# Backward layer-norm rows from x as loaded, with the scheduler's costs rewritten

## The chip, the cores and the metric

The kernel runs on one core of one Trainium2 chip. The metric is the device time of one execution in microseconds (us), lower is better. All engine names are those of the profile: PE is TensorE's matmul, PEld its weight load, DVE is VectorE, ACT is ScalarE, POOL is GpSimd, SP is SyncE.

## The reference

The reference computes a block of two residual layers and all its gradients. With x of 2048 rows (S) by 448 columns (D), in bfloat16:

```python
h  = x + irfft2(rfft2(layernorm(x)) * (w_r + 1j * w_i))     # a 2-D FFT filter over (S, D)
h2 = h + (gelu(layernorm(layernorm(h)).T @ w1 + b1) @ w2 + b2).T   # an MLP along S, F = 1792
return h2, *vjp(grad_out)     # gradients of x, w_r, w_i, w1, b1, w2, b2
```

What matters here is the gradient through the layer norm of x. With g the gradient that comes out of the inverse FFT for one row, r = 1/std and m the mean of that row of x, and n = (x - m) * r its normal form, the gradient of x is

```
gx = r * g  -  r * n * sum(g * n) / D  +  (gradient of the residual)
```

(the mean of g is zero here, because the table `di1` of the inverse transform leaves the constant term out).

## The kernel before

The program is not written in its final order. Every step is handed to a planner, `Plan`, as an operation with the engines it may run on, a planned occupation and a planned latency in us, the buffers that it reads and the buffers that it writes. `Plan.order()` runs a list schedule over all operations with these planned durations: at each step it takes the engine that can start something first, and of the operations that could start there the one with the longest path behind it (a `boost` adds to that length). `Plan.emit()` then writes each engine's instructions in the order found. On the chip each engine runs its own list strictly in order and waits by semaphores, so a planned duration that differs from the real one does not change what is computed, but an engine may then stand at an instruction whose input is late while later ones could have run. The numbers in the code that look like durations (`("DVE", 0.69, 0.77)`, `small()`, `mm()`) are these planned costs; they are not measured by the program.

Buffers come from rings. A ring has a number of slots; an operation that needs a new buffer can only be placed when a slot is free. `k1` (9 slots of one row tile, 128 x 448 bf16) serves the short-lived row tiles; `f2` (3 slots, float32) the copies out of PSUM; `hx` (3 slots) the reloaded rows of x and h; `ps` is the 8 banks of PSUM, with a limit for each kind of use (`sp` 5, `mm` 4, `mw` 8).

The stages, in the order in which they come: x is loaded and normalised (`Norm.stats`, `Norm.close`, `Norm.make`), transformed by rows (`fft_rows`) and by columns (`fft_cols`), multiplied with the filter (`cmul`), and transformed back (`ifft_cols`, `ifft_rows`), which gives h; h is normalised on POOL (`nh.alts`). The MLP follows (the products `ps_mg`, `ps_mp` and, backward, `ps_mm<-du,w1T`). Then the gradient of h goes through `norm_back` row tile by row tile (16 tiles, h = 0 to 15), and the backward FFT runs: `fft_rows`, `fft_cols`, `cmul`, `ifft_cols`, and in the last row loop (L1258) `ifft_rows` and `norm_back` for each of the 16 row tiles. The matmuls of the weight gradients (`ps_mm<-goT,g_t`, gradient of w2, and `ps_mw<-du_t,hlnT`, gradient of w1) depend on nothing in the backward FFT; the planner lays them between its steps.

The last row loop is where the largest part of the change lies. For each row tile it loads x again (`xr`, ring `hx`), turns it into its normal form in place with `nx.make` on POOL (L1262, the instruction itself is L745), takes the inverse transform (`odd` on ACT L939, two `eo` steps on DVE L941 and L943, six matmuls on PE), and calls `norm_back` (L1177):

- L1180, DVE: the product of g, in PSUM, with the normal form, summed over the row and scaled by `rneg` (r times -1/D) into the column `nm2`. The products go to a tile `junk` of ring `k1` that nobody reads. A small instruction that reads the accumulator follows it.
- L1193, ACT: `v` = r * g, from PSUM. (For the rows of h, L1186 and L1189: DVE makes a mean column `nm1`, ACT makes `v` = r * g + nm1.)
- L1196, DVE: `junk` = normal form * nm2 + v.
- L1199, DVE: the result = junk + the residual's gradient.

The columns r and shift (-m * r) of a norm stand in two arrays, `rstd` and `nb`; `Norm.factors` (L750) makes `rneg`. In the forward rows the row sum of h goes to a column `sm` of its own (L1005) and from there to `mv` (L710).

Of the kernel before, what the change touches and what calls it, by code (L numbers as in the profile page):

```python
# [401 lines left out]
def mm(*cols):  # L402
    t = sum(0.002 + 0.4215e-3 * max(n, 64) for n in cols)
    return [("PE", t, t + 0.07)]
# [3 lines left out]
def kernel(  # L408
# [35 lines left out]
    ring("k1", 9, fifo=False)  # L444
# [199 lines left out]
    rstd_x, rstd_h = const("rstd_x", [P, NT], F32), const("rstd_h", [P, NT], F32)  # L644
    nb_x, nb_h = const("nb_x", [P, NT], F32), const("nb_h", [P, NT], F32)
# [19 lines left out]
    class Norm:  # L665
        def __init__(self, nm, src, dst, by, rstd, nb, rneg, scale, eps, back, mirrored=()):
            self.nm, self.src, self.rstd, self.nb, self.rneg = nm, src, rstd, nb, rneg
            self.scale, self.eps, self.back = scale, eps, back
            self.dst, self.by = dst, by
            self.mirrored = mirrored  # L670

        alts = [("DVE", 0.305, 0.39), ("ACT", 0.65, 0.76)]

        def stats(self, h):
            bs = col(6, f"bs_{self.nm}")
            if h % self.by == 0:
                self.mv = col(2 * self.by, f"mv_{self.nm}")
            mv, i, n = self.mv, h % self.by, self.by
            pl.op(on_dve(448, 1.0e-3, 0.07), lambda e, on: e.bn_stats(out=bs[:], in_=self.src[:, h, :]),
                  r=[(self.src, h)], w=[bs])  # L680
            pl.op(small(), lambda e, on: e.bn_aggr(out=mv[:, 2 * i:2 * i + 2], in_=bs[:]), r=[bs], w=[(mv, i)])
            if i == n - 1:
                self.close(h, mv, self.scale)

        def close(self, h, mv, scale):
            n = self.by
            sl = slice(h + 1 - n, h + 1)
            hs = range(h + 1 - n, h + 1)
            v = col(n, f"v_{self.nm}")
            pl.op([("ACT", 0.19, 0.25)], lambda e, on: e.activation(  # L690
                out=v[:], in_=mv[:].rearrange("p (i c) -> p i c", c=2)[:, :, 1], func=ACT.Sqrt, bias=self.eps[:],
                scale=scale), r=[mv, self.eps], w=[v])
            pl.op(small(), lambda e, on: e.reciprocal(out=self.rstd[:, sl], in_=v[:]),
                  r=[v], w=[(self.rstd, k) for k in hs])
            pl.op(small(), lambda e, on: e.scalar_tensor_tensor(  # L695
                out=self.nb[:, sl], in0=mv[:].rearrange("p (i c) -> p i c", c=2)[:, :, 0], scalar=-1.0,
                in1=self.rstd[:, sl], op0=ALU.mult, op1=ALU.mult), r=[mv] + [(self.rstd, k) for k in hs],
                w=[(self.nb, k) for k in hs])
# [6 lines left out]
        def moments(self, h, sm):  # L705

            if h % self.by == 0:
                self.mv = col(2 * self.by, f"mv_{self.nm}")
            mv, i = self.mv, h % self.by
            pl.op(small(), lambda e, on: e.tensor_scalar(out=mv[:, 2 * i:2 * i + 1], in0=sm[:], scalar1=1.0 / D,  # L710
                                                         scalar2=None, op0=ALU.mult), r=[sm], w=[(mv, (i, 0))])
            sq = k1([P, D], "sq")
            pl.op([("ACT", 0.64, 0.8)], lambda e, on: e.activation(
                out=sq[:], in_=self.src[:, h, :], func=ACT.Square, scale=-1.0, bias=mv[:, 2 * i:2 * i + 1],
                accum_out=mv[:, 2 * i + 1:2 * i + 2]), r=[(self.src, h), (mv, (i, 0))], w=[sq, (mv, (i, 1))])
            if i == self.by - 1:
                self.close(h, mv, self.scale / D)

        def make_mirrored(self, h):

            for k in range(2):
                def go(e, on, k=k):
# [4 lines left out]
                    if on == "ACT":  # L727
                        e.activation(out=out, in_=in_, func=ACT.Identity, scale=self.rstd[:, h:h + 1],
                                     bias=self.nb[:, h:h + 1])
                    else:  # L730
                        e.tensor_scalar(out=out, in0=in_, scalar1=self.rstd[:, h:h + 1], scalar2=self.nb[:, h:h + 1],
                                        op0=ALU.mult, op1=ALU.add)
                pl.op([("DVE", 0.2, 0.28), ("ACT", 0.4, 0.5)], go, r=[(self.src, h), (self.rstd, h), (self.nb, h)],
                      w=[(self.dst, (h, k) if k else h)])

        def make(self, dst, h, src=None, at=None):
            s, i = (self.src, h) if src is None else (src, at)
            j = h if src is None else at

            def go(e, on):  # L740
                if on == "ACT":
                    e.activation(out=dst[:, j, 0:D], in_=s[:, i, :], func=ACT.Identity,
                                 scale=self.rstd[:, h:h + 1], bias=self.nb[:, h:h + 1])
                else:
                    e.tensor_scalar(out=dst[:, j, 0:D], in0=s[:, i, :], scalar1=self.rstd[:, h:h + 1],  # L745
                                    scalar2=self.nb[:, h:h + 1], op0=ALU.mult, op1=ALU.add)

            pl.op(self.alts, go, r=[(s, i), (self.rstd, h), (self.nb, h)], w=[(dst, j)])

        def factors(self):  # L750
            pl.op(small(), lambda e, on: e.tensor_scalar(out=self.rneg[:], in0=self.rstd[:], scalar1=self.back,
                                                         scalar2=None, op0=ALU.mult),
                  r=[self.rstd], w=[self.rneg])
# [129 lines left out]
    def ifft_cols(ys, ab):  # L883

        for a in (7, 6, 5, 4, 3, 2, 1, 8):
# [16 lines left out]
            matmuls([pa, pb], calls, rd + [hi], mm(*[128] * (len(calls) // 2)), "rows")  # L902
# [80 lines left out]
    nx = Norm("x", x, xln, 4, rstd_x, nb_x, rneg_x, 1.0, eps_x, -1.0 / D, (0,))  # L983
# [16 lines left out]
    nh = Norm("h", hn, hln, 2, rstd_h, nb_h, rneg_h, 1.0 + LN_EPS, eps_h, -(1.0 + LN_EPS) / D)  # L1000
    nh.alts = [("POOL", 0.95, 1.05)]
    for h in range(NT):
        with grouped():
            py = ifft_rows(ab, di0, h)
            sm = col(1, "sm")  # L1005
            pl.op([("DVE", 0.61, 0.69)], lambda e, on, py=py, h=h, sm=sm: e.tensor_tensor_reduce(
                out=hn[:, h, :], in0=py[:], in1=hn[:, h, :], scale=1.0, scalar=0.0, op0=ALU.add, op1=ALU.add,
                accum_out=sm[:]), r=[py, (hn, h)], w=[(hn, h), sm])
            nh.moments(h, sm)
# [51 lines left out]
    for j in range(NFB):  # L1061
# [28 lines left out]
        gop(on_dve(448, 1.2e-3, 0.07), [kk, hh], [(du, j), (gb1, j)], lambda e, g, j=j: e.scalar_tensor_tensor(  # L1090
# [69 lines left out]
    for t in range(NT):  # L1160
# [3 lines left out]
        pl.op(on_dve(448), lambda e, on, t=t, p2=p2, h2=h2: e.scalar_tensor_tensor(  # L1164
# [5 lines left out]
    for h in range(NT):  # L1170
        pl.op([("ACT", 0.55, 0.65)], lambda e, on, h=h: e.activation(
# [5 lines left out]
    def norm_back(pb, mean, xhat, xkey, h, nm, base, out, okey):  # L1177
        nm2 = col(1, "nm2")
        junk = k1([P, D], "junk")
        pl.op([("DVE", 0.69, 0.77)], lambda e, on: e.tensor_tensor_reduce(  # L1180
            out=junk[:], in0=pb[:, 0:D], in1=xhat(), scale=nm.rneg[:, h:h + 1], scalar=0.0, op0=ALU.mult,
            op1=ALU.add, accum_out=nm2[:]), r=[pb, xkey, nm.rneg], w=[junk, nm2])
        v = pl.buf("f2", [P, D], "v", F32)
        if mean:
            nm1 = col(1, "nm1")
            pl.op(small(), lambda e, on: e.tensor_scalar(  # L1186
                out=nm1[:], in0=pb[:, D:D + 1], scalar1=nm.rstd[:, h:h + 1], scalar2=-1.0 / D, op0=ALU.mult,
                op1=ALU.mult), r=[pb, (nm.rstd, h)], w=[nm1])
            pl.op([("ACT", 0.6, 0.7)], lambda e, on: e.activation(  # L1189
                out=v[:], in_=pb[:, 0:D], func=ACT.Identity, scale=nm.rstd[:, h:h + 1], bias=nm1[:]),  # L1190
                r=[pb, nm1, (nm.rstd, h)], w=[v])
        else:
            pl.op([("ACT", 0.53, 0.63)], lambda e, on: e.activation(  # L1193
                out=v[:], in_=pb[:, 0:D], func=ACT.Copy, scale=nm.rstd[:, h:h + 1]),
                r=[pb, (nm.rstd, h)], w=[v])
        pl.op(on_dve(448, 1.1e-3), lambda e, on: e.scalar_tensor_tensor(  # L1196
            out=junk[:], in0=xhat(), scalar=nm2[:], in1=v[:], op0=ALU.mult, op1=ALU.add), r=[xkey, nm2, v, junk],
            w=[junk])
# [17 lines left out]
    for h in range(NT):  # L1216
        pd = product("mm", D + 1, [(lambda h=h, j=j: w1T[h][0][:, w1T[h][1], j, :], lambda j=j: du[:, j, 0:D + 1],
                                    [w1T[h], (du, j), (du, (j, 1))]) for j in range(NFB)], [P, 512])
        norm_back(pd, True, lambda h=h: hln[:, h, :], (hln, h), h, nh, lambda h=h: go_r[:, h, :],
# [162 lines left out]
```

## Time and profile before

| | |
|---|---|
| runs | 354.47, 354.40, 352.72 us; median 354.40 us |
| the profiled execution | 352.68 us, its span 350.9 us |
| granted TensorE clock | 1.00 |
| PE busy | 329.8 us, 94% of the span |
| DVE busy | 275.0 us, 78% |
| ACT busy | 191.4 us, 55% |
| POOL busy | 83.7 us, 24% |

The span runs from the first to the last instruction; the 1.8 us between it and the execution's time lie around it. The profiled execution lies at the low end of the runs. The page's busy time of PE is the time in which at least one matmul was under way, and its idle time is what is left.

### The profile page before, as it was taken

What the parts mean: (1) busy time and instruction counts of PE and PEld (TensorE: products, weight loads), DVE (VectorE), ACT (ScalarE), POOL (GpSimd) and SP (SyncE); (2) the same over time, 40 slices, a digit from 0 to 9 for tenths busy, and PEclk for the clock granted to TensorE, in tenths of its full rate; (3) what the DMA queues carried; (4) which work ended last, traced back from release to release, by engine and by line L of the source; (5) the groups of instructions that cost most, each with busy time, mean ns of one, the idle gap of its engine ahead of it and who ended that gap; (6) DMA issues with size and microseconds to landing.
All of it is one profiled execution on the core that took longest, in us unless ns stands there. A gap on an engine that the chain in (4) does not pass through costs nothing. (4 is left out here: it accounts for less than half of the span.)

```text
span 350.9 us, 6872 instructions
## 1 busy us (share of the span) xinstructions
PE 329.8 (94%) x2507; PEld 179.8 (51%) x2507; DVE 275.0 (78%) x747; ACT 191.4 (55%) x410; POOL 83.7 (24%) x140
## 2 busy tenths in 40 slices
PE   0979999999999999999999999998999999899994
PEld 0546555677555555555555555654556555444441
DVE  5898999899379994323277887989997989998852
ACT  2596843486487776406012323976878676634332
POOL 0000000056701101033220100050111566355642
PEclk9999999999999999999999999999999999999999
DMA  7999999994999999799799999999996546347755
GB/s 238 384 222 216 179 179 288 223 244 139 358 302 282 355 279 346 182 348 239 194 222 239 186 226 239 225 184 164 150 171 217 178 175 219 143 174 241 220 196 209
DMA packets 134685, 80.49 MB, mean 229 GB/s; under 512 B 94268, under 2 KB 127164, under 8 KB 134524
## 3 DMA queue, kind: packets, MB, share of 16 engines
q1 hardware_dynamic: 127148, 52.71, 70.8%
q0 software_dynamic: 7504, 27.35, 23.3%
q8 instruction: 19, 0.31, 0.4%
q14 instruction: 14, 0.11, 0.1%
HBM read 30.98 MB, written 27.08 MB: 165 GB/s over the span
## 5 line engine op out<-in xcount | busy, mean ns | idle before, releaser
L517 PE MATMUL ps_mm<-goT,g_t 128*128 128x512 bf16 x224 | 55.6, 379 | 0.8 <-DVE nm L1180 0.8
L517 PE MATMUL ps_mg<-go_n,w2T 128*128 128x448 bf16 x224 | 50.3, 357 | 0.8 <-DMA go_n<-in_grad_out_dram 0.8
L517 PE MATMUL ps_mw<-du_t,hlnT 128*128 128x448 bf16 (+1 forms) x256 | 45.4, 353 | 0.5 <-DVE nm L1180 0.3
L517 PE MATMUL ps_mm<-du,w1T 128*128 128x449 bf16 x224 | 43.3, 353 | 0.0
L517 PE MATMUL ps_mp<-hln,w1c 128*128 128x448 bf16 x224 | 42.7, 352 | 0.0
L517 PE MATMUL ps_mp<-gT,w2c 128*128 128x448 bf16 x224 | 42.7, 352 | 0.0
L507 ACT CAST s<-ps_mm 128x512 bf16<-128x512 f32 x56 | 33.1, 602 | 9.7 <-PE ps_mm L517 9.6
L499 POOL DMA_DIRECT2D out_dram<-s x31 | 17.1, 552 | 86.5 <-ACT s L507 70.1
L1189 ACT ACTIVATE v<-ps_mm,nm,rstd_h 128x448 f32<-128x448 f32 x16 | 11.6, 726 | 42.4 <-DVE nm L1186 42.4
L517 PEld LDWEIGHTS <-hlnT 128*128 128x128 bf16 (+1 forms) x256 | 20.5, 97 | 23.8 <-issue 6.6
L517 PEld LDWEIGHTS <-w1T 128*128 128x128 bf16 x224 | 21.8, 97 | 21.1
L517 PEld LDWEIGHTS <-w2c 128*128 128x128 bf16 x224 | 21.9, 98 | 20.5
L517 PEld LDWEIGHTS <-w1c 128*128 128x128 bf16 x224 | 21.9, 98 | 20.5
L507 ACT CAST s<-ps_mw 128x448 bf16<-128x448 f32 x32 | 16.3, 535 | 24.9 <-PE ps_mw L517 22.6
L517 PEld LDWEIGHTS <-g_t 128*128 128x128 bf16 x224 | 19.4, 97 | 19.5 <-issue 2.4
L517 PEld LDWEIGHTS <-w2T 128*128 128x128 bf16 x224 | 19.6, 98 | 15.8 <-issue 1.7
L509 DVE CAST s<-ps_mw 128x448 bf16<-128x448 f32 x32 | 19.2, 620 | 8.8 <-PE ps_mw L517 3.7
L1164 DVE SCALAR_TENSOR_TENSOR h<-ps_mp,b2c,hr 128x448 bf16<-128x448 f32 x16 | 9.8, 677 | 16.6 <-PE ps_mp L517 16.6
L817 DVE TENSOR_TENSOR gg<-ps_sp,gb 128x226 bf16<-128x226 f32 x60 | 20.0, 408 | 3.2 <-ACT gb L507 3.2
L499 POOL DMA_DIRECT2D hn_d<-x x4 | 2.4, 590 | 73.4 <-DVE nb_h L695 72.5
L1077 DVE SCALAR_TENSOR_TENSOR ge<-ge 128x448 bf16<-128x448 bf16 x14 | 8.7, 621 | 14.1 <-ACT ge L1075 14.1
L517 PEld LDWEIGHTS <-kinv 128*128 128x128 bf16 x192 | 14.8, 97 | 8.2 <-DVE eo L943 3.5
(128 smaller groups left out, 590.1 us busy)
## 6 DMA issues: line engine op xcount, KB each, us to landing
w2c<-in_B_w_dram SPq DMA_DIRECT2D x8, 896.0 KB, 9.0
out_dram<-s POOLq DMA_DIRECT2D x14, 512.0 KB, 4.8
out_dram<-s POOLq DMA_DIRECT2D x15, 448.0 KB, 3.0
w1c<-in_B_w_dram SPq DMA_DIRECT2D x6, 1024.0 KB, 11.5
x<-in_A_x_dram SPq DMA_DIRECT2D x4, 448.0 KB, 6.7
go_n<-in_grad_out_dram SPq DMA_DIRECT2D x2, 896.0 KB, 10.6
hn_d<-x POOLq DMA_DIRECT2D x4, 448.0 KB, 6.1
hln_d<-hln POOLq DMA_DIRECT2D x4, 448.0 KB, 7.4
```

The lines of the kernel that those rows point to most:

```text
L499: e.dma_start(out=out() if callable(out) else out, in_=in_())
L507: e.copy(out=out(), in_=in_())
L509: e.tensor_copy(out=out(), in_=in_())
L517: e.matmul(out(), lhsT=lhsT(), rhs=rhs(), start=start, stop=stop)
L817: pl.op(on_dve(226), lambda e, on, s_=s_, op=op: e.tensor_tensor(out=g_[:, s_, :].rearrange("p (k t) -> p t k", t=2), in0=pr[:, 0:2, :], i ...
L1077: gop(stt, [q_, uf], [zz], lambda e, g: e.scalar_tensor_tensor(out=g(zz), in0=g(q_), scalar=6.0 * GELU_C, in1=g(uf), op0=ALU.add, op1=ALU. ...
L1164: pl.op(on_dve(448), lambda e, on, t=t, p2=p2, h2=h2: e.scalar_tensor_tensor(out=h2[:], in0=p2[:, 0:D], scalar=b2c[:, t:t + 1], in1=hr[t / ...
L1189: pl.op([("ACT", 0.6, 0.7)], lambda e, on: e.activation(out=v[:], in_=pb[:, 0:D], func=ACT.Identity, scale=nm.rstd[:, h:h + 1], bias=nm1[: ...
```

## The change

The change has four parts.

1. In the last row loop the normal form of x is no longer made. `norm_back` takes x as loaded. Because the mean of g is zero, sum(g * n) = r * sum(g * x), so `factors` multiplies `rneg` of x by r once more (one instruction for the whole kernel). The column c = sum(g * x) * rneg is then multiplied with the pair (r, shift), which now stand side by side in one array `rn`, by one small DVE instruction on 128 x 2 values; ACT makes v = r * g + shift * c with the function Identity in place of Copy, and DVE adds x * (r * c).
2. The row-sum products (`junk`) get a ring of their own, `jk`, of 2 slots; `k1` goes from 9 slots to 8.
3. `rstd` and `nb` are merged into `rn`; the square root's column becomes a part of `mv`, and so does the row sum `sm` of the forward rows. No instruction is added or removed by this.
4. Planned costs are rewritten: of short matmuls, of the `rows` matmuls of `ifft_cols`, of the row sums, of the fused multiply-adds, of the normalisation on POOL, and of the row sums on ACT. The four sign copies of the table `kf` at the start get a boost of 60.

```diff
 def mm(*cols):
-    t = sum(0.002 + 0.4215e-3 * max(n, 64) for n in cols)
+    t = sum(0.002 + 0.4215e-3 * max(n, 120) for n in cols)
...
-    ring("k1", 9, fifo=False)
+    ring("k1", 8, fifo=False)
+    ring("jk", 2, fifo=False)
...
-            matmuls([pa, pb], calls, rd + [hi], mm(*[128] * (len(calls) // 2)), "rows")
+            matmuls([pa, pb], calls, rd + [hi], mm(*[143] * (len(calls) // 2)), "rows")
...
         def factors(self):
-            pl.op(small(), lambda e, on: e.tensor_scalar(out=self.rneg[:], in0=self.rstd[:], scalar1=self.back,
+            pl.op(small(), lambda e, on: e.tensor_scalar(out=self.rneg[:], in0=self.rn[:, :, 0], scalar1=self.back,
...
+            if self.raw:
+                pl.op(small(), lambda e, on: e.tensor_tensor(out=self.rneg[:], in0=self.rneg[:], in1=self.rn[:, :, 0],
+                                                             op=ALU.mult), r=[self.rn, self.rneg], w=[self.rneg])
...
+    pl.boost = 60.0
     for k, sign in ((1, 1.0), (2, -1.0), (3, -1.0), (4, 1.0)):
-        pl.op([("DVE", 0.1, 0.2)], lambda e, on, k=k, sign=sign: e.tensor_scalar(
+        pl.op([("DVE", 0.118, 0.2)], lambda e, on, k=k, sign=sign: e.tensor_scalar(
             out=kf[:, k, :], in0=kf[:, 0, :], scalar1=sign, scalar2=None, op0=ALU.mult), r=[(kf, 0)], w=[(kf, k)])
+    pl.boost = 0.0
...
+    nx.raw = True
...
-    nh.alts = [("POOL", 0.95, 1.05)]
+    nh.alts = [("POOL", 0.72, 0.78)]
...
-            pl.op([("DVE", 0.61, 0.69)], lambda e, on, py=py, h=h, sm=sm: e.tensor_tensor_reduce(
+            pl.op([("DVE", 0.54, 0.68)], lambda e, on, py=py, h=h, mv=mv, i=i: e.tensor_tensor_reduce(
...
-        pl.op(on_dve(448), lambda e, on, t=t, p2=p2, h2=h2: e.scalar_tensor_tensor(
+        pl.op([("DVE", 0.595, 0.68)], lambda e, on, t=t, p2=p2, h2=h2: e.scalar_tensor_tensor(
...
-        pl.op([("ACT", 0.55, 0.65)], lambda e, on, h=h: e.activation(
+        pl.op([("ACT", 0.70, 0.80)], lambda e, on, h=h: e.activation(
...
-    def norm_back(pb, mean, xhat, xkey, h, nm, base, out, okey):
-        nm2 = col(1, "nm2")
-        junk = k1([P, D], "junk")
-        pl.op([("DVE", 0.69, 0.77)], lambda e, on: e.tensor_tensor_reduce(
+    def norm_back(pb, xhat, xkey, h, nm, base, out, okey):
+        nms = col(3, "nm")
+        junk = pl.buf("jk", [P, D], "junk")
+        pl.op([("DVE", 0.605, 0.73)], lambda e, on: e.tensor_tensor_reduce(
             out=junk[:], in0=pb[:, 0:D], in1=xhat(), scale=nm.rneg[:, h:h + 1], scalar=0.0, op0=ALU.mult,
...
-        if mean:
...
-            pl.op([("ACT", 0.6, 0.7)], lambda e, on: e.activation(
-                out=v[:], in_=pb[:, 0:D], func=ACT.Identity, scale=nm.rstd[:, h:h + 1], bias=nm1[:]),
+        if nm.raw:
+            by = 1
+            pl.op([("DVE", 0.075, 0.17)], lambda e, on: e.tensor_scalar(
+                out=nms[:, 1:3], in0=nm.rn[:, h, :], scalar1=nms[:, 0:1], scalar2=None, op0=ALU.mult),
+                r=[(nms, 0), (nm.rn, (h, 0)), (nm.rn, (h, 1))], w=[(nms, 1), (nms, 2)])
         else:
-            pl.op([("ACT", 0.53, 0.63)], lambda e, on: e.activation(
-                out=v[:], in_=pb[:, 0:D], func=ACT.Copy, scale=nm.rstd[:, h:h + 1]),
+            by = 0
+            pl.op([("DVE", 0.131, 0.213)], lambda e, on: e.tensor_scalar(
+                out=nms[:, 2:3], in0=pb[:, D:D + 1], scalar1=nm.rn[:, h, 0:1], scalar2=-1.0 / D, op0=ALU.mult,
...
-        pl.op(on_dve(448, 1.1e-3), lambda e, on: e.scalar_tensor_tensor(
-            out=junk[:], in0=xhat(), scalar=nm2[:], in1=v[:], op0=ALU.mult, op1=ALU.add), r=[xkey, nm2, v, junk],
+        pl.op([("ACT", 0.53, 0.64)], lambda e, on: e.activation(
+            out=v[:], in_=pb[:, 0:D], func=ACT.Identity, scale=nm.rn[:, h, 0:1], bias=nms[:, 2:3]),
+            r=[pb, (nms, 2), (nm.rn, (h, 0))], w=[v])
+        pl.op([("DVE", 0.595, 0.68)], lambda e, on: e.scalar_tensor_tensor(
+            out=junk[:], in0=xhat(), scalar=nms[:, by:by + 1], in1=v[:], op0=ALU.mult, op1=ALU.add),
...
     gx_op = []
-    nx.alts = nh.alts
     for h in range(NT):
         with grouped():
             py = ifft_rows(ab2, di1, h)
             g = h // 2
-            nx.make(xr[g], h, xr[g], h % 2)
             gx = k1([P, D], "gx")
-            norm_back(py, False, lambda g=g, h=h: xr[g][:, h % 2, :], (xr[g], h % 2), h, nx,
+            norm_back(py, lambda g=g, h=h: xr[g][:, h % 2, :], (xr[g], h % 2), h, nx,
```

More of the change, by code (lines that the diff above doesn't have):

```diff
@@ L642, in ld_w1 @@
                      w1v[:, :, a * P:b_ * P], P * NT * (b_ - a) * P * 2)
-    rstd_x, rstd_h = const("rstd_x", [P, NT], F32), const("rstd_h", [P, NT], F32)
-    nb_x, nb_h = const("nb_x", [P, NT], F32), const("nb_h", [P, NT], F32)
+    rn_x, rn_h = const("rn_x", [P, NT, 2], F32), const("rn_h", [P, NT, 2], F32)
     rneg_x, rneg_h = const("rneg_x", [P, NT], F32), const("rneg_h", [P, NT], F32)
@@ L688, in close @@
             hs = range(h + 1 - n, h + 1)
-            v = col(n, f"v_{self.nm}")
             pl.op([("ACT", 0.19, 0.25)], lambda e, on: e.activation(
[L691 to L694, printed above, removed]
+                out=mv[:, 2 * n:3 * n], in_=mv[:, 1:2 * n:2], func=ACT.Sqrt, bias=self.eps[:],
+                scale=scale), r=[mv, self.eps], w=[(mv, "v")])
+            pl.op(small(), lambda e, on: e.reciprocal(out=self.rn[:, sl, 0], in_=mv[:, 2 * n:3 * n]),
+                  r=[(mv, "v")], w=[(self.rn, (k, 0)) for k in hs])
             pl.op(small(), lambda e, on: e.scalar_tensor_tensor(
-                out=self.nb[:, sl], in0=mv[:].rearrange("p (i c) -> p i c", c=2)[:, :, 0], scalar=-1.0,
-                in1=self.rstd[:, sl], op0=ALU.mult, op1=ALU.mult), r=[mv] + [(self.rstd, k) for k in hs],
-                w=[(self.nb, k) for k in hs])
+                out=self.rn[:, sl, 1], in0=mv[:, 0:2 * n:2], scalar=-1.0,
+                in1=self.rn[:, sl, 0], op0=ALU.mult, op1=ALU.mult), r=[mv] + [(self.rn, (k, 0)) for k in hs],
+                w=[(self.rn, (k, 1)) for k in hs])
             for k in hs:
@@ L727, in go @@
                     if on == "ACT":
-                        e.activation(out=out, in_=in_, func=ACT.Identity, scale=self.rstd[:, h:h + 1],
-                                     bias=self.nb[:, h:h + 1])
+                        e.activation(out=out, in_=in_, func=ACT.Identity, scale=self.rn[:, h, 0:1],
+                                     bias=self.rn[:, h, 1:2])
                     else:
-                        e.tensor_scalar(out=out, in0=in_, scalar1=self.rstd[:, h:h + 1], scalar2=self.nb[:, h:h + 1],
+                        e.tensor_scalar(out=out, in0=in_, scalar1=self.rn[:, h, 0:1], scalar2=self.rn[:, h, 1:2],
@@ L732, in go, with make @@
                                         op0=ALU.mult, op1=ALU.add)
-                pl.op([("DVE", 0.2, 0.28), ("ACT", 0.4, 0.5)], go, r=[(self.src, h), (self.rstd, h), (self.nb, h)],
+                pl.op([("DVE", 0.25, 0.34), ("ACT", 0.46, 0.57)], go, r=[(self.src, h), (self.rn, (h, 0)), (self.rn, (h, 1))],
                       w=[(self.dst, (h, k) if k else h)])
-        def make(self, dst, h, src=None, at=None):
-            s, i = (self.src, h) if src is None else (src, at)
-            j = h if src is None else at
+        def make(self, dst, h):
@@ L740, in go @@
             def go(e, on):
                 if on == "ACT":
-                    e.activation(out=dst[:, j, 0:D], in_=s[:, i, :], func=ACT.Identity,
-                                 scale=self.rstd[:, h:h + 1], bias=self.nb[:, h:h + 1])
-                else:
-                    e.tensor_scalar(out=dst[:, j, 0:D], in0=s[:, i, :], scalar1=self.rstd[:, h:h + 1],
-                                    scalar2=self.nb[:, h:h + 1], op0=ALU.mult, op1=ALU.add)
-            pl.op(self.alts, go, r=[(s, i), (self.rstd, h), (self.nb, h)], w=[(dst, j)])
+                    e.activation(out=dst[:, h, 0:D], in_=self.src[:, h, :], func=ACT.Identity,
+                                 scale=self.rn[:, h, 0:1], bias=self.rn[:, h, 1:2])
+                else:
+                    e.tensor_scalar(out=dst[:, h, 0:D], in0=self.src[:, h, :], scalar1=self.rn[:, h, 0:1],
+                                    scalar2=self.rn[:, h, 1:2], op0=ALU.mult, op1=ALU.add)
@@ L999 @@
     hln = big(1, [P, NT, D], "hln")
[L1000 to L1001 removed]
+    nh = Norm("h", hn, hln, 2, rn_h, rneg_h, 1.0 + LN_EPS, eps_h, -(1.0 + LN_EPS) / D)
+    nh.alts = [("POOL", 0.72, 0.78)]
     for h in range(NT):
@@ L1181, in norm_back @@
             out=junk[:], in0=pb[:, 0:D], in1=xhat(), scale=nm.rneg[:, h:h + 1], scalar=0.0, op0=ALU.mult,
-            op1=ALU.add, accum_out=nm2[:]), r=[pb, xkey, nm.rneg], w=[junk, nm2])
+            op1=ALU.add, accum_out=nms[:, 0:1]), r=[pb, xkey, nm.rneg], w=[junk, (nms, 0)])
         v = pl.buf("f2", [P, D], "v", F32)
-        if mean:
[L1185 to L1188, printed above, removed]
-            pl.op([("ACT", 0.6, 0.7)], lambda e, on: e.activation(
-                out=v[:], in_=pb[:, 0:D], func=ACT.Identity, scale=nm.rstd[:, h:h + 1], bias=nm1[:]),
-                r=[pb, nm1, (nm.rstd, h)], w=[v])
-        else:
-            pl.op([("ACT", 0.53, 0.63)], lambda e, on: e.activation(
-                out=v[:], in_=pb[:, 0:D], func=ACT.Copy, scale=nm.rstd[:, h:h + 1]),
-                r=[pb, (nm.rstd, h)], w=[v])
```

39 lines of the change are left out of this document (21 added, 18 removed).

## The prediction

> **What bounds the kernel.** I read the page's busy times first: PE is the engine that is nearly full, and DVE is the next.
>
> ```profile
> PE 329.8 (94%) x2507; PEld 179.8 (51%) x2507; DVE 275.0 (78%) x747; ACT 191.4 (55%) x410; POOL 83.7 (24%) x140
> ```
>
> The chain that ended last says little more (its last long piece is 26.52 us of PE's `ps_mw`), so the question is where PE stood still. Going through PE's timeline, I add up the gaps between matmuls: the first 8.43 us (waiting for `w2n`'s transfer), then 8.08 us in all. They lie in four places: 2.76 us in the start (0.76 before 11.08, 2.00 before 23.20), 0.83 in the forward column transform, 1.53 around 240, and 2.94 from 275 to 316, in the last row loop. Everything else is matmuls end to end, and 4.6 us behind the last matmul are eviction and store. So an edit is worth what it takes out of these gaps, and no more.
>
> Next I asked for the timeline of each engine around the gap at 240. First PE, then DVE, then POOL:
>
> ```profile
> 238.77 0.38 PE L517 MATMUL ps_sp<-gg,hf 128*64 128x225 bf16 x4
> 240.47 0.69 PE L517 MATMUL ps_sp<-gg,hf 128*64 128x225 bf16 x8 [1.32 <-DVE gg L817]
> ...
> 242.50 0.35 PE L517 MATMUL ps_sp<-gg,hf 128*64 128x225 bf16 x3 [0.21 <-DVE gg L817]
> ```
>
> ```profile
> 233.77 3.34 DVE L860 TENSOR_TENSOR t_r<-ds,w_b 128x1800 bf16<-128x1800 bf16 x1
> 237.03 1.08 DVE L860 TENSOR_TENSOR t_i<-ds,w_b 128x1800 bf16<-128x1800 bf16 x1
> 238.04 1.01 DVE L817 TENSOR_TENSOR gg<-ps_sp,gb 128x226 bf16<-128x226 f32 x3
> ```
>
> ```profile
> 231.95 4.21 POOL L745 TENSOR_SCALAR xr<-xr,rstd_x,nb_x 128x448 bf16<-128x448 bf16 x6
> ```
>
> The same product (`t_r`, `t_i`, 128x1800) takes 3.34 us while POOL is making the normal form of x, and 1.08 us right after. PE waits for a DVE result 1.32 + 0.21 us behind it. Comparing every DVE instruction with the median of its group, I find two more that overlap POOL's L745, both in the last row loop:
>
> ```profile
> 297.00 1.31 DVE L1199 TENSOR_TENSOR gx<-junk,go_r 128x448 bf16<-128x448 bf16 x1
> ```
>
> ```profile
> 297.07 1.67 POOL L745 TENSOR_SCALAR xr<-xr,rstd_x,nb_x 128x448 bf16<-128x448 bf16 x2
> ```
>
> This `gx` takes 1.31 us where its neighbours take 0.38. The third is an L1196 at 282.62 with 0.80 for 0.68. Together POOL's 16 normalisations cost DVE 2.26 + 0.93 + 0.12 = 3.31 us. The chain that ended last runs straight through the second one:
>
> ```profile
> 298.31 0.30 DVE eo L943
> ...
> 300.93 0.09 DVE nm L1180
> 301.02 0.04 issue
> 301.06 1.89 PE ps_mm L517 x8
> ```
>
> The `eo` that PE waits for stands behind the blocked `gx`; PE loses 0.21 us before 298.67 and 0.75 before 301.06.
>
> **The change, part by part.** *POOL's normal form goes (16 x 0.712 us of POOL).* POOL itself is 24% busy and costs nothing; what counts is what DVE gets back. At 240: 1.53 us of PE's idle time. At 297: 0.21 + 0.75 = 0.96. Sum -2.49 us. Why it should reach the end: PE has a fixed amount of matmuls to do, and from 242 to 346 its gaps add up to 3.2 us, so what starts earlier ends earlier. What is late next at 240 is the other input of that matmul, ACT's copy `gb`, and it was itself waiting for DVE (2.34 us idle before 240.50), so it moves up too.
>
> [...]
>
> *One small DVE instruction more for each row tile (128x2).* Nearest rows: `RECIPROCAL rstd_h`, 128x2, lasts 160 ns, but what the queue loses is the distance to the next start, 0.07 to 0.12 us (22.51 to 22.59, 22.88 to 22.94). 16 x 0.08 = 1.3 us of DVE, at most 16 x 0.16 = 2.6. From 270 to 308 DVE is busy 34.6 of 38 us, so it's not free: it gets back 1.05 us there from POOL, so the net is +0.25 us (+1.5 at most). As DVE's own relief there is counted above through PE's gap, I charge +0.2.
>
> [...]
>
> *ACT's `v` now waits for DVE.* Before, L1193 needed PSUM alone and ran beside L1180. Now the row is a chain: L1180 (0.61 to the next start, 0.08 for the accumulator) then the small one (0.15), then `v`, then L1196. Queued behind `v` on ACT are the `odd` copies and the evictions of `ps_mm`, for which PE waits. `v` itself goes from Copy to Identity with a bias column: L1193 has 639 ns, L1189, the same function on the same shape, 724: 16 x 0.085 = 1.4 us of ACT, which is 70% busy there (26 of 38 us), so hidden. The wait is hidden if another row's `eo`, L1196 or L1199 is there for DVE and evictions for ACT: a row period is 2.6 us (L1180 from 270.62 to 309.28 in 15 steps) and the row's chain from L1180 to L1199 some 3.1 us, so two rows must be in flight. The planner knows the dependency and two `jk` slots allow just that. Cost between 0 and 16 x 0.6 us; the nearest row is L1189 itself, which already stands in such a chain in the rows of h with no PE gap; I take +0.3.
>
> *Rings and columns.* `k1` loses a slot but gives up `junk`, of which two were alive at a time: 0. The columns: the same instructions, 0. `factors`: one instruction of 0.17 us for the kernel, 0.
>
> *The start.* The sign copies of `kf` move from behind the second statistics (9.12 to 12.14) to the moment the table lands. They cost DVE 4 x 0.12 us, of which half now sits in the wait after a reciprocal: at most +0.5. In return PE can begin `kf,xln` when the first row is ready (about 10.3 in place of 12.52), without the 0.76 us wait; ACT's `zt` copies and, queued behind them, `v_x` (17.69, DVE idle 1.51 us for it) come earlier, and with them the `w` for which PE stood 2.00 us. Between -2.3 and +0.5; I take -0.5, as `go_n` and `w2T` may hold PE anyway.
>
> *Planned costs.* Each comes nearer to the trace: four 113-column matmuls take 0.21 us (planned 0.198, now 0.210), L1180 0.61 (0.69, now 0.605), L1196 0.60 (0.56, now 0.595), POOL 0.71 (0.95, now 0.72). A better plan should leave fewer of the remaining gaps (0.83 in the columns, 1.98 in the row loop), but a new order is a new draw. -1.5 to +1.5; taken as 0.
>
> Sum: -2.49 + 0.2 + 0.3 - 0.5 = -2.5 us. On the profiled 352.68 that is 350.2; counted from the median of the runs, 354.40, it is 351.9. The profiled execution lies at the low end of the runs (352.72 to 354.47), and a new median may fall anywhere between, so I say 351.0, in the middle.
>
> **Rivals.**
>
> *The new wait shows (slower).* In the last row loop ACT stands at `v` until DVE has done L1180 and the small column, the `odd` copies behind it come late, `eo` is late, and PE stalls as it already does five times on `eo`. For: two of 16 `v` waited for DVE already (1.5 us). Against: PE has `ps_mw` to fill with, ACT has 30% to spare. If half the rows lose 0.76 + 0.15 us, that's 8 x 0.91 = 7.3, less the 2.5 gained: 352.7 + 4.8 = 357.5. It decides from 3 rows in 16, where 2.7 eats the gain. If five rows are hit, 4.5 - 2.5 = +2.0: 354.7 from the profiled time, 356.4 from the median.
>
> *The lock is gone but nothing arrives.* The gap at 240 closes, but the planner places other work so that PE waits elsewhere, for DVE that has 1.3 us more to do: a gain of 0 to 1.5 from the middle of the two times (353.5): 352.0 to 353.5. For: DVE is 91% busy in the row loop and the order is drawn anew. Against: PE's gap at 240 has one cause, which is gone.
>
> *The start and the better plan pay in full.* -2.49 - 2.3 and another -1 in the row loop, 5.8 in all: 346.9 from the profiled time, 348.6 from the median.
>
> **How the numbers follow.** About 0.5% (1.8 us) is what a measurement of this kernel can tell from no change. The forecast has 0.5, the full gain 0.1, the lock with nothing to show 0.2, the slower one 0.2. Faster takes the first two: 0.6; same 0.2; slower 0.2. The range: the forecast's own is 349 to 353 (the new order 1.5 us each way, the spread of the runs 0.9); the lower end goes to 348.5 for half of the full gain, the upper to 355.5 to take in the slower case with a few rows hit.
>
> **What would show it.** Right: no L745 `xr`; `t_r<-ds,w_b` 128x1800 at about 1.08 us; all L1199 near 0.38; no PE gap over 0.5 us between 230 and 270; 16 small DVE instructions that cost 0.08 each. Wrong: ACT idle before `v` with PE waiting on `eo` for more than the 1.5 us of before in the row loop; PE's gaps over the whole span adding up to 8 us or more again; a gap in the start that grew because DVE did `kf` before its statistics.

## The result, and the profile after

The changed kernel takes 354.79 us (median of 22 executions, 353.76 to 357.71); the kernel before, run beside it on the same chip, 353.07 us (22 executions, 351.92 to 355.84). The ratio is 1.0051 with a 95% interval of 1.0032 to 1.0070: slower by 0.5%, where a gain of 2.5 us was forecast. The profiled execution of after takes 354.65 us with a span of 352.9 us, 2.0 us longer than the span before. The ratios leave out executions over 1.5% above the fastest of the same kernel: three of six of `e3_raw_only` below, one of twelve of `e1_own_column`, no others.

The busy times on the page say that work did move as intended: POOL lost 12.0 us and DVE 4.6 us, and PE still fills 94% of a longer span.

```profile
PE 331.7 (94%) x2507; PEld 180.6 (51%) x2507; DVE 270.4 (77%) x755; ACT 196.8 (56%) x419; POOL 71.7 (20%) x124
```

Where the prediction expected relief, relief came. The groups by form show `t_r` at 1.10 us (3.34 before), `gx` at a mean of 394 ns (442 before), and the new small instruction (columns: busy us, mean ns of one, idle time before):

```profile
L859 DVE TENSOR_TENSOR t_r<-ds,w_b 128x1800 bf16<-128x1800 bf16 x1 | 1.1, 1097 | 0.0
...
L1206 DVE TENSOR_TENSOR gx<-junk,go_r 128x448 bf16<-128x448 bf16 x16 | 6.2, 394 | 0.0
...
L1192 DVE TENSOR_SCALAR nm<-rn_x,nm 128x2 f32<-128x2 f32 x16 | 3.7, 232 | 0.0
```

From 266 to 304, in the last row loop, PE is busy 37.92 of 38 us (35.52 before), and all of PE's gaps behind 226 add up to 0.67 us. Yet PE's gaps behind its first matmul sum to 7.93 us over the whole span, almost the 8.08 of before. What was won at 240 and in the row loop was lost in a place where before had no gap at all. First PE's timeline of before, where the same products follow each other without a wait:

```profile
220.16 0.39 PE L517 MATMUL ps_sp<-kf,w 128*113 128x128 bf16 x4
220.38 0.59 PE L517 MATMUL ps_mm<-goT,g_t 128*128 128x512 bf16 x2
220.81 0.39 PE L517 MATMUL ps_sp<-kf,w 128*113 128x128 bf16 x4
```

And PE's timeline of after; the bracket gives the idle time before an instruction and what ended it:

```profile
220.18 0.38 PE L518 MATMUL ps_sp<-kf,w 128*113 128x128 bf16 x4 [0.16 <-ACT v L1200]
222.89 0.59 PE L518 MATMUL ps_mm<-goT,g_t 128*128 128x512 bf16 x2 [2.33 <-ACT v L1200]
223.37 0.53 PE L518 MATMUL ps_sp<-kf,w 128*113 128x128 bf16 x4
225.59 1.01 PE L518 MATMUL ps_mm<-goT,g_t 128*128 128x512 bf16 x2 [1.69 <-ACT v L1200]
226.39 0.63 PE L518 MATMUL ps_sp<-kf,w 128*113 128x128 bf16 x4
226.82 4.47 PE L518 MATMUL ps_mm<-goT,g_t 128*128 128x512 bf16 x12
```

Two long gaps, 2.33 and 1.69 us, and with the 0.16 ahead of them 4.18 us in all, each ended by `v` (L1200). This is not the `v` of the last row loop, which the prediction feared: it belongs to the rows of h, 50 us earlier, whose code the change hardly touches. Behind the gaps, 12 matmuls take 4.47 us, 0.37 each. The windows of after show why (columns: PE, PEld, DVE, ACT, POOL busy with counts, granted clock, DMA share, GB/s):

```profile
218.00:222.00 4.00, 2.40 (x29) 1.85 (x28) 3.05 (x10) 0.72 (x1) 0.00 (x0) 1.00 0.75 211
222.00:226.00 4.00, 1.42 (x8) 0.73 (x8) 3.09 (x8) 2.39 (x5) 0.00 (x0) 0.68 0.00 0
226.00:229.00 3.00, 3.00 (x12) 1.42 (x11) 3.00 (x9) 2.19 (x6) 0.00 (x0) 0.50 0.49 97
229.00:232.00 3.00, 3.00 (x24) 1.74 (x23) 1.53 (x6) 2.20 (x5) 0.00 (x0) 0.79 1.28 290
```

The granted clock, 1.00 here before, falls to half. So the loss goes on after the gap: in the kernel with the mended plan (`e2_planner_told`) 14 of the same matmuls take 3.18 us, 0.227 each, and 12 x (0.372 - 0.227) = 1.7 us.

Landmarks give the sum. The first matmul starts 0.27 later (8.43 to 8.70); from there to the end of the last `ps_mm<-du,w1T` it is 210.12 before and 210.20 after, +0.08; from there to the end of the last backward `kf,w` 8.76 and 15.04, +6.28; from there to the last matmul 119.05 and 114.40, -4.65. Together +1.98, the difference of the spans to within 0.03.

### The profile page after: what moved, and what is told of

Read it like the earlier page. It is cut to its first block, busy times and chain, and to the rows that moved or that the text cites. A ratio compares the mean times of both kernels' runs of the same rounds, so it can differ in the third digit from the quotient of the medians.

```text
span 352.9 us, 6853 instructions
## 1 busy us (share of the span) xinstructions
PE 331.7 (94%) x2507; PEld 180.6 (51%) x2507; DVE 270.4 (77%) x755; ACT 196.8 (56%) x419; POOL 71.7 (20%) x124
## 5 line engine op out<-in xcount | busy, mean ns | idle before, releaser
L518 PE MATMUL ps_mm<-goT,g_t 128*128 128x512 bf16 x224 | 56.8, 391 | 4.0 <-ACT v L1200 4.0
L518 PE MATMUL ps_mg<-go_n,w2T 128*128 128x448 bf16 x224 | 49.4, 355 | 1.6 <-DMA go_n<-in_grad_out_dram 0.7
L1200 ACT ACTIVATE v<-ps_mm,nm,rn_h 128x448 f32<-128x448 f32 x16 | 11.6, 725 | 48.7 <-DVE nm L1186 46.7
L518 PEld LDWEIGHTS <-g_t 128*128 128x128 bf16 x224 | 20.3, 100 | 25.3 <-issue 7.4
L508 ACT CAST s<-ps_mw 128x448 bf16<-128x448 f32 x38 | 18.6, 538 | 22.9 <-PE ps_mw L518 19.3
L510 DVE CAST s<-ps_mw 128x448 bf16<-128x448 f32 x26 | 15.9, 624 | 10.2 <-PE ps_mw L518 8.3
L1203 DVE SCALAR_TENSOR_TENSOR junk<-hln,nm,v 128x448 bf16<-128x448 bf16 x16 | 10.9, 684 | 11.8 <-ACT v L1200 11.8
```

Of the source, the lines that this page charges most:

```text
L508: e.copy(out=out(), in_=in_())
L510: e.tensor_copy(out=out(), in_=in_())
L518: e.matmul(out(), lhsT=lhsT(), rhs=rhs(), start=start, stop=stop)
L1200: pl.op([("ACT", 0.53, 0.64)], lambda e, on: e.activation(out=v[:], in_=pb[:, 0:D], func=ACT.Identity, scale=nm.rn[:, h, 0:1], bias=nms[:, ...
L1203: pl.op([("DVE", 0.595, 0.68)], lambda e, on: e.scalar_tensor_tensor(out=junk[:], in0=xhat(), scalar=nms[:, by:by + 1], in1=v[:], op0=ALU. ...
```

## Why PE waits at 220

The chain of waits stops at `v`; the question is why `v` is late. In the rows of h, each row tile needs on DVE a row sum, a mean column and, behind ACT's `v`, a fused multiply-add and an addition. DVE also folds finished rows (`u`, `w`, L770 before and L769 after) into the input of `kf,w`. DVE's timeline of before, one row:

```profile
210.71 0.68 DVE L1180 CUSTOM_DVE_ANT_0 junk<-ps_mm,hln,rneg_h 128x448 bf16<-128x448 f32 x1
...
211.45 1.15 DVE L770 TENSOR_TENSOR u<-go_r 128x896 bf16<-128x896 bf16 x2
212.51 0.68 DVE L1196 SCALAR_TENSOR_TENSOR junk<-hln,nm,v 128x448 bf16<-128x448 bf16 x1
...
213.53 0.68 DVE L1180 CUSTOM_DVE_ANT_0 junk<-ps_mm,hln,rneg_h 128x448 bf16<-128x448 f32 x1
```

And a row of after, first on DVE and then ACT's `v` of that row:

```profile
211.97 0.67 DVE L1186 CUSTOM_DVE_ANT_0 junk<-ps_mm,hln,rneg_h 128x448 bf16<-128x448 f32 x1
...
213.53 0.69 DVE L1203 SCALAR_TENSOR_TENSOR junk<-hln,nm,v 128x448 bf16<-128x448 bf16 x1 [0.88 <-ACT v L1200]
214.25 0.39 DVE L1206 TENSOR_TENSOR go_r<-junk,go_r 128x448 bf16<-128x448 bf16 x1
214.68 1.16 DVE L769 TENSOR_TENSOR u<-go_r 128x896 bf16<-128x896 bf16 x2
215.76 0.21 DVE L1197 TENSOR_SCALAR nm<-ps_mm,rn_h 128x1 f32<-128x1 f32 x1
215.88 0.68 DVE L1186 CUSTOM_DVE_ANT_0 junk<-ps_mm,hln,rneg_h 128x448 bf16<-128x448 f32 x1
```

```profile
212.77 0.73 ACT L1200 ACTIVATE v<-ps_mm,nm,rn_h 128x448 f32<-128x448 f32 x1 [1.99 <-DVE nm L1186]
```

In both, some 0.9 us pass between the row sum and the multiply-add, because `v` runs only after the row sum. Before lays the fold `u` in that hole: a row with a fold takes 2.82 us. After leaves the hole empty, waits 0.88 us, and lays the fold between rows: such a row takes 3.91 us. The starts of the 16 row sums of h span 40.53 us before (178.44 to 218.97) and 45.12 us after (178.91 to 224.03). The product that feeds them ends at 218.55 and 218.90. So before is done with the rows as the product ends, and after is two rows behind; by the brackets above, PE's next products start only behind the `v` of those rows, after 0.16, 2.33 and 1.69 us, which fits PSUM banks that the rows still hold.

The order differs because the plan does. In `order()` the longest path behind an operation counts occupations. By the old costs, mean column and `v` (0.075 + 0.60 = 0.675) are shorter than the row sum (0.69), so the row sum comes first and the plan itself sees the hole. By the new ones 0.131 + 0.53 = 0.661 is longer than 0.605: the mean column comes first, and the plan lets `v` run beside the row sum, so that it sees no hole to fill. On the chip `v` doesn't run beside it. The dependency that keeps it back isn't among those the planner was given. (The new costs of row sum and mean column are closer to the trace than the old ones. That of `v` isn't: where ACT goes straight on, its next start comes 0.62 us behind `v`, from 222.12 to 222.74, so 0.60 was the nearer number. With it the sum would be 0.731 and the order the same.)

## The experiments

**Is it the shared column tile?** After puts row sum and mean into one tile, `nms`; before had two. Theory A: `v` waits for the row sum because of the tile. Theory B: it waits whatever the tile.

```diff
-            by = 0
+            by, nm1 = 0, col(1, "nm1", bufs=2)
...
-                out=nms[:, 2:3], in0=pb[:, D:D + 1], ...
+                out=nm1[:], in0=pb[:, D:D + 1], ...
```

The ring of `nms` goes from four columns to three, and `v` takes its bias from the new column; every engine's order is that of after.

> The changed kernel with one edit: in the rows of h the mean column is written to a tile of its own instead of the third column of the tile that L1186's accumulator also writes. Every engine's instructions stay in the same order; only what `v` (L1200) waits for changes. Theory A (the shared tile): `v` waited for L1186 because both columns lie in one tile; with its own column it starts about 0.25 us after the row's product is done in place of 0.9, the DVE row chain goes from 2.72 us to some 2.1, under the 2.67 of the product, so it no longer falls behind; the PE gaps of 2.33 and 1.69 us before the backward FFT and the twelve slow matmuls behind them (1.9 us) go: about 6 us, 347 to 350 us against 353.1 of before. Rival B (two slots for the row-sum products, or the folds placed between the rows): the rows stay at 2.7 us each, the gaps stay, 354 to 355.

Measured: 356.26 us against 354.0 of before, ratio 1.0062 (1.0024 to 1.0099). The gaps stay (0.13 + 2.33 + 1.26). DVE's mean column and row sum, then ACT's `v`, in the timelines of this kernel:

```profile
220.57 0.21 DVE L1197 TENSOR_SCALAR nm<-ps_mm,rn_h 128x1 f32<-128x1 f32 x1
220.70 0.67 DVE L1186 CUSTOM_DVE_ANT_0 junk<-ps_mm,hln,rneg_h 128x448 bf16<-128x448 f32 x1
```

```profile
221.50 0.72 ACT L1200 ACTIVATE v<-ps_mm,nm,rn_h 128x448 f32<-128x448 f32 x1 [1.99 <-DVE nm L1186]
```

The column that `v` reads is made ahead of 220.70, in a tile of its own, and `v` still starts after the row sum. Theory A falls.

**Does it help if the planner knows?** After, with one entry changed in the list of what `v` reads. The instruction and its waits on the chip are the same; the plan now puts `v` behind the row sum.

```diff
-            r=[pb, (nms, 2), (nm.rn, (h, 0))], w=[v])
+            r=[pb, nms, (nm.rn, (h, 0))], w=[v])
```

> The changed kernel with the shared tile kept, but the planner told of it: `v` is listed as reading the whole tile, so the plan has `v` behind L1186. The order changes, the wait remains. Theory A in its full form (not the wait as such, but a plan that does not know of it): the folds go into the wait for `v` as in the kernel before, the last rows of h are not late, PE gaps before the backward FFT under 1 us, 349 to 352 us. If the wait as such is the cost: the rows still fall behind, 354 to 355. Rival B (two slots): as slow as the changed kernel.

Measured: 349.79 us against 354.0, ratio 0.9887 (0.9844 to 0.9931). The fold is back in the hole, in DVE's timeline of this kernel, and the row starts span 40.84 us (178.06 to 218.90):

```profile
210.64 0.68 DVE L1186 CUSTOM_DVE_ANT_0 junk<-ps_mm,hln,rneg_h 128x448 bf16<-128x448 f32 x1
...
211.38 1.15 DVE L769 TENSOR_TENSOR u<-go_r 128x896 bf16<-128x896 bf16 x2
212.44 0.67 DVE L1203 SCALAR_TENSOR_TENSOR junk<-hln,nm,v 128x448 bf16<-128x448 bf16 x1
```

The gap on PE is gone but for 0.11 us and the clock stays at 1.00. `e11_told_again` is the same kernel once more, run beside another experiment:

> e2 once more, unchanged, on the same chip as e10, to compare with. 348 to 350.5 us.

It measured 349.08 against 352.56, 0.9882 (0.9837 to 0.9928). One true dependency in the plan is worth 1.6% (1.0051 to 0.9887).

**By the mean's cost alone.** If the order flipped over 0.661 against 0.605, setting the mean column's occupation back should do as well.

```diff
-            pl.op([("DVE", 0.131, 0.213)], lambda e, on: e.tensor_scalar(
+            pl.op([("DVE", 0.070, 0.213)], lambda e, on: e.tensor_scalar(
```

> The changed kernel with one planned number altered: the mean column of the rows of h (L1197) at 0.070 us of occupation in place of 0.131. Its path (0.070 + 0.53 for `v`) is then shorter than the row sum's 0.605, so the plan puts the row sum first again, as in the kernel before, and `v` behind both. Theory C (DVE's row sum and ACT's `v` read the same PSUM bank and so run one after the other in the order in which they were written; the plan doesn't know, and the new costs made it count on `v` running beside the row sum): the plan is true again, PE gaps before the backward FFT under 1 us, 348.5 to 351 us against 353.5 of before. Rival (the other new costs, or the ring of two slots, hold the rows up): gaps of 3 us or more stay, 355 to 357.

Measured: 349.25 against 353.13, ratio 0.9896 (0.9859 to 0.9933); gaps 0.25 + 0.11 in place of 4.18, row starts over 41.1 us. A planned number that is 0.06 us too low undoes the loss, because it puts the row sum first again.

**What holds `v` back on the chip.** DVE's row sum and `v` read the same PSUM tile. Here `v` of the rows of h takes its input from SBUF (the normal form `hln` stands in for g, so that term is left out of the gradient). The order of every engine is that of `e1_own_column`.

```diff
-            out=v[:], in_=pb[:, 0:D], func=ACT.Identity, ...
+            out=v[:], in_=pb[:, 0:D] if nm.raw else hln[:, h, :], func=ACT.Identity, ...
```

> e1 (the changed kernel with the mean column in a tile of its own, every engine's order unchanged) with `v` in the rows of h reading the normal form of h from SBUF instead of the product in PSUM; the gradient through h's norm is left out that way. Theory C: nothing in PSUM is shared any more, `v` starts when the mean column is there, beside the row sum; DVE's wait of 0.88 us for `v` in each row goes, the rows take at most 2.2 us, the two PE gaps near 220 (3.6 to 4.0 us) go: 347 to 350 us. Rival (it waits for the row sum for another reason: ring slots, DVE's own order): `v` still starts 0.9 us behind, gaps stay, 354 to 357.

Measured: 347.33 against 353.13, ratio 0.9854 (0.9812 to 0.9895). First ACT's timeline, then DVE's:

```profile
213.87 0.76 ACT L1200 ACTIVATE v<-hln,nm,rn_h 128x448 f32<-128x448 bf16 x1 [1.39 <-DVE nm L1197]
```

```profile
213.67 0.68 DVE L1186 CUSTOM_DVE_ANT_0 junk<-ps_mm,hln,rneg_h 128x448 bf16<-128x448 f32 x1
...
214.66 0.68 DVE L1203 SCALAR_TENSOR_TENSOR junk<-hln,nm,v 128x448 bf16<-128x448 bf16 x1 [0.31 <-ACT v L1200]
```

`v` is released by the mean column (L1197) and runs beside the row sum, as the plan had it; the hole shrinks from 0.88 to 0.31, the row starts span 40.2 us, and there is no gap at 220. Over the 16 rows of h, row sum and `v` never overlap in `e1_own_column`; here they do in 15. With the same order, it is the common PSUM tile that keeps `v` back: while both read it they run one after the other, 0.80 us from start to start in `e1_own_column` (220.70 to 221.50), and 0.20 here (213.67 to 213.87). For that row of `e1_own_column` the profile names the row sum's accumulator (L1186) as what ended ACT's wait of 1.99 us. It infers that from semaphore events, so the wait stands in the built program, while the list that the planner works from doesn't have it. (`v` reads the tile until 222.22 there, 0.85 us behind the row sum, and not at all here, so the tile can also come free earlier and the whole gain isn't the wait's alone.)

**The two halves of the change.** `e4_costs_only` is before with only the new planned costs and the boost; `e3_raw_only` is before with only x as loaded (no new costs, no ring `jk`).

The costs, two of some fifteen lines:

```diff
-        pl.op([("DVE", 0.69, 0.77)], lambda e, on: e.tensor_tensor_reduce(
+        pl.op([("DVE", 0.605, 0.73)], lambda e, on: e.tensor_tensor_reduce(
...
-            pl.op([("ACT", 0.6, 0.7)], lambda e, on: e.activation(
+            pl.op([("ACT", 0.53, 0.64)], lambda e, on: e.activation(
```

> The kernel before with the new planned costs and the boost of `kf`, nothing else. Theory A: the plan now puts the mean column ahead of the row sum and counts on an early `v`; here the mean has its own tile, so `v` is early, nothing falls behind; the blocked `t_r` and `gx` remain in some form: 352 to 354. Rival (the new costs themselves bring the loss): PE gaps of 3 us or more between 218 and 230, 355 to 357.

Measured: 357.28 against 354.0, ratio 1.0113 (1.0066 to 1.0160), with the gaps 2.33 + 1.82 at 220 to 225. Mean and row sum have tiles of their own here, which speaks once more against theory A. The new order also happened to keep POOL's normal form away from `t_r` (1.10 us), and the kernel is slower all the same. And x as loaded alone:

```diff
-            nx.make(xr[g], h, xr[g], h % 2)
...
+            nm2x = col(2, "nm2x")
+            pl.op([("DVE", 0.075, 0.17)], lambda e, on: e.tensor_scalar(
+                out=nm2x[:], in0=rnx[:, h, :], scalar1=acc[:], scalar2=None, op0=ALU.mult),
```

> The kernel before with x as loaded in the last row loop and nothing else: no normalisation on POOL, one small DVE instruction for each row, `v` behind the row sum; old costs, old rings, old columns (the pair of columns is copied into one tile once). The prediction's step: t_r at 1.08 us, the PE gap of 1.53 near 240 gone, no 1.31 us gx, -2.5 us: 350 to 351.5. Its rival (the new wait of `v` shows): PE gaps in the last row loop over 4 us, 353 to 357.

Measured: ratio 0.9880 (0.9815 to 0.9944), from three executions (347.76 to 351.39). The other three took 355.26 to 357.98, and the median of all six is 353.32 against 354.0, so this ratio is weak evidence. The profiled execution is one of the long ones (355.74). From the first matmul to the end of the `w1T` product it takes 216.16 us where before takes 210.12; PE waits 2.69 us at 150, where before doesn't wait. From there to the last matmul it takes 125.01 us, before 127.81: 2.80 less, and this is the stretch in which x as loaded acts. So the planned costs, with the boost, made the kernel slower. X as loaded made its own stretch shorter; that the kernel as a whole is faster by it alone rests on three executions.

**The relief of DVE with a sound plan.** `e4_costs_only` with the dependency told for both kinds of rows; POOL's normal form is kept. Beside `e2_planner_told` it shows what x as loaded brings (with the ring `jk` and the merged columns).

```diff
-                r=[pb, (nm.rstd, h)], w=[v])
+                r=[pb, nm2, (nm.rstd, h)], w=[v])
```

> The kernel before with the new planned costs and boost (as in e4) and the plan told, for both kinds of rows, that `v` comes behind the row sum; POOL's normalisation of x is kept. Against e4 it shows what the truth in the plan is worth, against e2 what x as loaded is worth. Theory C with the prediction's price for the lock: no gap near 220 (4 us less than e4), but DVE instructions over 1 us longer where they meet POOL: 350.5 to 353, 1 to 2.5 above e2. Rival (x as loaded is worth nothing, all of e2's gain is the plan): equal to e2 within 0.7 us.

Measured: 350.98 against 353.13, ratio 0.9945 (0.9914 to 0.9975). `t_r` again stretches over POOL's run (POOL's timeline, then DVE's), and PE has its 1.46 us gap at 240 again:

```profile
233.57 4.19 POOL L745 TENSOR_SCALAR xr<-xr,rstd_x,nb_x 128x448 bf16<-128x448 bf16 x6
```

```profile
235.40 3.31 DVE L860 TENSOR_TENSOR t_r<-ds,w_b 128x1800 bf16<-128x1800 bf16 x1
```

From 0.9945 to 0.9887 x as loaded is worth 0.6%, about 2 us. The two intervals overlap, so this size is rough. In the stretch where it acts, from the end of the last backward `kf,w` to the last matmul, the traces have 116.21 us here and 114.72 in `e2_planner_told`, 1.49 less.

**The ring.** `e2_planner_told` with `junk` back in `k1` of 9 slots.

```diff
-    ring("k1", 8, fifo=False)
-    ring("jk", 2, fifo=False)
+    ring("k1", 9, fifo=False)
```

> e2 (the changed kernel, the plan told that `v` comes behind the row sum) with the row-sum products back in ring `k1` of 9 slots. Prediction's step (the ring costs nothing): equal to e2 within 1 us, 349 to 351. Rival (two slots hold back the rows in the last row loop): 1 us or more faster.

Measured: 348.79 against 353.13, ratio 0.9893 (0.9856 to 0.9930), the same as with the ring. It is worth nothing that this measurement can tell.

**The start.** `e2_planner_told` without the boost of the four sign copies.

```diff
-    pl.boost = 60.0
```

> e2 (the changed kernel, the plan told that `v` comes behind the row sum) without the boost of the four copies of `kf`, so that they stand where the kernel before has them. It prices the prediction's step on the start (-0.5 us, bounds -2.3 and +0.5). If that step holds, this is 0.5 us or more slower than e2 of the same call, and the PE gaps before 24 us add up to 0.3 us or more above e2's 2.5. Rival (the start is bound by the arrival of x and by DVE, whatever the order of `kf`): equal within 0.5 us.

Measured: 353.93 against 352.56, ratio 1.0031 (0.9999 to 1.0063); with the boost, on the same chip, 0.9882. `kf,xln` starts at 19.35 in place of 12.23. But PE doesn't lose its time there: from the first matmul to the end of the `w1T` product it takes 214.15 us in place of 210.39, and the waits between 60 and 96 us name the place, where PE stands 2.43 and 1.03 us for a transfer:

```profile
PE ps_mg L518 <- DMA w2T<-in_B_w_dram: 3.5, 2, 2.4
```

With the new costs the boost is worth 4.85 us in the medians (353.93 against 349.08), and 3.76 of that shows in the profiled executions by the end of the `w1T` product, through the order of work 60 us later. Why the transfer comes late there was not settled.

## Why the prediction was wrong, point by point

*Lock relief, -2.49:* right in its cause, and somewhat high in size. With no normal form on POOL `t_r` takes 1.10 us in place of 3.34, and no `gx` takes over 0.41 where one took 1.31; by what means POOL holds DVE up, which the prediction calls a lock, no run shows. The gap at 240 and the row loop's waits on the blocked `gx` went; with a sound plan x as loaded is worth about 2 us in the ratios and 1.49 us in its own stretch.

*Small instruction, +0.2 from 16 x 0.08:* mis-sized. It lasts 232 ns and the next start comes 0.13 us behind it: 16 x 0.13 = 2.1 us of DVE, inside the bound of 2.6. It is hidden all the same: PE is busy 37.92 of 38 us in the row loop.

*`v` behind DVE, +0.3:* nothing shows in the row loop, but the reasoning failed. "Before, L1193 needed PSUM alone and ran beside L1180" was wrong: in the row loop of before none of the 16 pairs overlaps. In 15 of them `v` went first. Where the two met, one waited for the other, and the waits of before said so (total us, times, longest):

```profile
ACT v L1193 <- DVE nm L1180: 1.5, 2, 0.9
...
DVE junk L1180 <- ACT v L1193: 1.1, 2, 0.6
```

In the code of before these two instructions share nothing but the PSUM tile that both only read, and yet within one row `v` waits 0.61 us for the row sum (before 281.95), and the row sum 0.60 and 0.55 us for `v` (before 277.02 and 287.18). I used the first line as a sign for the rival and overlooked what the pair means: in this kernel these two reads of one PSUM tile are kept apart. "The planner knows the dependency" held for the rows of x, where the new small column makes it true, and not for the rows of h.

*Planned costs, taken as 0 (-1.5 to +1.5):* this is the step that failed. Together with the boost they cost 1.1% (`e4_costs_only`, 3 to 4 us), more than twice the upper bound. I argued that "each comes nearer to the trace" makes a plan better. That held for the costs I listed, though not for `v`'s, but nearer numbers don't make a better plan when a dependency is missing: the old wrong numbers kept the row sum first by 0.015 us, and so hid the missing dependency. I compared single costs with the trace and never asked which pairs of paths in the plan would change places. With the dependency told, the same costs and boost make before faster by 0.55% (`e8_told_pool_kept`).

*The start, -0.5:* +0.1 measured from before to after to the end of the `w1T` product, within the bounds. What the boost does is larger and elsewhere (`e10_told_no_kf_boost`).

*Rings and columns, 0:* right (`e9_told_junk_k1`, `e1_own_column`).

*The rivals:* the slower one named the right instruction, `v` behind DVE, with the time of 354.7 for a few rows hit, but in the last row loop and through the new wait. `e2_planner_told` keeps that wait and is fast, so the match with the measured 354.79 is luck. It is luck, too, that 354.79 lies under the range's upper end of 355.5, which was set for this rival. "PE waits elsewhere, the order is drawn anew" came nearest to what happened, with a price too small (0 to 1.5).

The sum thus reads: -2 us from x as loaded, some +4 from planned costs and boost in a plan that lacks a dependency; after is 1.7 us slower in the medians. `e2_planner_told` beats both kernels: 1.1% faster than before.

What stays open: whether telling the dependency to the plan of before, with its old costs, would bring something (not run); and how much of the two gaps each held PSUM bank accounts for.

## What to carry to other kernels

Where a planner orders the work, a corrected cost is an edit of the order: find the pairs of paths whose lengths change places, and look in the trace at whether the two operations that the plan now sets side by side ever ran side by side. A wait between two instructions that only read the same PSUM tile is such a sign, and it stands in the waits of before (0.61, 0.60 and 0.55 us). Give the planner the dependency before giving it better durations.

## What the runs showed of the hardware

In after the granted clock of PE halves behind two gaps, 2.33 and 1.69 us: PE is busy 1.42 of 4 us from 222 to 226, and the granted clock from 226 to 229 is 0.50. In `e10_told_no_kf_boost` gaps of 2.43 and 1.03 us leave it at 1.00, with PE busy 1.98 of 4 us from 84 to 88. Neither the longest gap nor the share of idle time settles it. From 18 to 23.20, before and the profiled execution of `e3_raw_only` run the same matmuls: each has one gap of 2.00 us and PE busy 3.20 of 5.20 us. Behind it the clock stays at 1.00 in before and falls to 0.50 in `e3_raw_only` (columns as in the windows above, first before, then `e3_raw_only`). What decides between the two was not found.

```profile
23.20:26.60 3.40, 3.40 (x30) 2.21 (x31) 3.40 (x12) 3.11 (x6) 0.00 (x0) 1.00 1.09 241
```

```profile
23.20:26.60 3.40, 3.40 (x21) 2.46 (x22) 2.84 (x9) 3.08 (x6) 0.00 (x0) 0.50 1.06 222
```

DVE's `t_r`, which has two SBUF inputs, became longer beside POOL. It takes 1.10 us in after, where POOL makes no normal form of x, 3.34 before and 3.31 in `e8_told_pool_kept`; both times it started while POOL was in a run of six instructions of 0.70 us and ended 0.95 us behind the last of them. That is nearly its whole length of 1.10 us, so by an estimate from these times it waited for more than one POOL instruction. The blocked `gx` of before did not wait for its run: it ended at 298.31, while POOL's two normalisations, begun at 297.07, lasted until 298.74, which is 0.25 us longer than two of 0.71. By the same kind of estimate DVE came through after the first there, and POOL's second was late. L1180, which has one input in PSUM, kept its 0.68 us beside POOL (at 277.02 and 287.18, within POOL's runs from 276.69 to 278.10 and from 286.91 to 288.32). Why `t_r` and `gx` differ was not settled.
